# Four sets of priorities for a planned instruction order, and later planned arrivals, in a fused sparse attention and MoE kernel

## The chip, the cores and the metric

The kernel runs on one core of one Trainium2 chip. The core has five engines with their own instruction queues, each worked off in order: TensorE (PE; its weight loads are shown apart as PEld), VectorE (DVE), ScalarE (ACT), GpSimd (POOL) and SyncE (SP). They wait for each other and for DMA transfers by semaphores. In this kernel POOL and SP issue the transfers. The metric is the device time of one execution in microseconds, the median of several runs; lower is better.

## The reference

Inputs are q, k and v of shape (8, 8, 576, 64): batch, heads, positions, width. Then come an input matrix of 512 x 2048 and an output matrix of 2048 x 512, and two scalars s and b.

```python
scores = scale * np.matmul(q, k.transpose(0, 1, 3, 2))
mask_local = (rel >= 0) & (rel < 32)
mask_strided = (rel >= 0) & (pos[None, :] % 32 == pos[:, None] % 32)
# heads 0 to 3 are local, heads 4 to 7 strided; softmax; times v
x = attn_out.transpose(0, 2, 1, 3).reshape(4608, 512)
h = x @ w_in
r = np.maximum(h, 0.0)
out = (s * (r * r) + b) @ w_out
```

rel is the distance between query and key position. The output is 4608 x 512 in float32.

## The kernel before

**Tiling.** The eight batches are taken one after the other. Each has four pairs of heads, m = 0 to 3; m = 0 and 1 are local (suffix l, `loc`), m = 2 and 3 strided (suffix s, `str`). Because of the masks only small blocks of scores are computed: 6 blocks of 96 queries for a local pair, 8 of 72 for a strided one. For a pair, `pair_steps` (L474) makes the steps: transposes of q and k (`trans`, L485; from some batch on they are DMA transposes instead, L555 to L582), scores (L610), the exponential on ACT (L641), the mask on DVE (L649), the product with v (`av`, L673), the reciprocal of the row sums (L701), the scaling (L711) and the transpose of the result x (`xtrans`, L727, or DMA transposes, L752 to L763). The result is `xT`, one tile for each m, with room for three batches.

The tokens are then taken in nine blocks of 512, T = 0 to 8. FF1 (`ff1`, L973) multiplies xT with w_in, 16 tiles of 4 matmuls a block, followed by a relu (`u`, L1009 or L1011) and a square (`gT`, L1017 or L1019). FF2 multiplies gT with w_out (`ff2`, L1229, for T = 0 and 1; from T = 2 on `ff2_seven`, L853, with seven products of half blocks in place of eight, on sums of gT and of w_out, `S` and `w_mix`). For T = 7 and 8 FF1 too uses seven products (`ff1_seven`, L1087), on sums of xT (`x_sum`, L1036) and of w_in (`w_sum`), with the products kept by copies V, U and E (L1113).

**The order of the work** is not left to the hardware or a scheduler. While the kernel is built, the class `Plan` (L19) keeps a planned time `plan.t` and writes every engine's program in the order in which it plans the work. PE's work is a list of `Step`s with a planned duration each. Work of the other engines is *posted* when the step that it follows is planned: a post has needs (names of results), a cost for each engine that can do it ("A" ACT, "V" DVE, "P" POOL, "D", "X" and "Y" transfers on SP) and the names that it makes. `flush` (L45) takes from the posts that are ready at `plan.t` the one with the smallest key, and puts it on the engine that would finish it first:

```python
w = r + self.LATER.get(k[0] if isinstance(k, tuple) and k[2:3] != (0,) else None, 0.0)
```

r is the time at which its needs are there, k the first name that it makes, and `LATER` is the table `ORDER` (L124): a number of nanoseconds for each kind of name, by which it stands later (or, negative, earlier) in the choice. A post whose engines are all taken for more than `SLACK` (600 ns) beyond `plan.t` is held back. The kinds: q and k are the spreading and copying of transposed q and k (`qD_loc`, `qD_str`, `kT_loc`, `kTs`), e the exponential, p the mask (in batch 0, where a matmul adds the mask, p is the exponential), r the reciprocal, x the scaling, u the relu, g the square, `in` the copies that make loaded q, k and v usable, S, w_mix, wc and xc the sums, ev the output of FF2; the rest (Va to C22, fv to c12) belong to the seven-product forms.

**What PE does next** is chosen in the loop at L1520. Among four pairs of heads from the first unfinished one it takes the first whose next step is ready, and puts it ahead of FF1 and FF2 as long as the attention work done is below `due()` (L1515), which follows the positions reached in FF1 and FF2 plus `ahead`:

```python
pos = f1_pos[i1] + (f2[i2 - 1].pos if i2 else 0.0) + plan.ahead
return (pos if pos <= 1 else 1 + (pos - 1) / 2) * batch_ns
```

`batch_ns` is the planned PE time of one batch of attention (that of batch 1). FF1 goes before FF2 unless it is more than 1 block ahead (L1538). Where nothing is ready, early in the program, `keep_running` (L1487, matmul at L1502) fills PE's time with matmuls on constants; later the planned time is simply moved on. Real waits are kept by semaphores, so a wrong planned time can't change a result, only the order.

**Loads.** POOL issues the loads of inputs and weights. `landing` (L1309) plans when a load is there: it adds the loads up one after the other, and at the end 600 ns, or 6000 ns after 60 us. `fetch_qk` (L1319) loads q and k, `fetch_v` (L1339) v of a batch: `load_vl` the local heads into `v_loc`, `early_v` or `load_vs` the strided ones. v_loc is followed by a copy of 32 rows for each half of the heads (`rows_before`, L435, in the trace "v_loc<-v_loc" at L404).

Of the kernel before, what the change touches and what calls it, by code (L numbers as in the profile page):

```python
# [1 line left out]

# [1 line left out]

# [1 line left out]

# [12 lines left out]
class Plan:  # L19
# [8 lines left out]

    def __init__(self, order):
        self.t = 0.0  # L30
        self.SLACK, self.ahead, self.LATER = order["SLACK"], order["ahead"], order
        self.done = {}
        self.pend = []
        self.free = {"A": 0.0, "V": 0.0, "P": 7000.0, "D": 0.0, "X": 0.0, "Y": 0.0}
        self.banks = {}

    def ready_at(self, needs):
        if any(k not in self.done for k in needs):
# [3 lines left out]
    def post(self, needs, cost, fn, keys, lat=None):  # L42
        self.pend.append((needs, cost, fn, keys, lat))

    def flush(self):  # L45
        while True:
            best = None
            for p in self.pend:
                r = self.ready_at(p[0])
                if r is None or r > self.t:  # L50
                    continue
                if p[1].keys() <= {"A", "V"} and min(
                        self.free[e] for e in p[1]) > self.t + self.SLACK:
                    continue
                k = p[3][0]
                w = r + self.LATER.get(k[0] if isinstance(k, tuple) and k[2:3] != (0,) else None, 0.0)
                if best is None or w < best[0]:
                    best = (w, r, p)
            if best is None:
                return  # L60
            _, r, p = best
            self.pend.remove(p)
            eng = min(p[1], key=lambda e: max(self.free[e], r) + p[1][e])
            end = max(self.free[eng], r, self.t - self.SLACK) + p[1][eng]
            self.free[eng] = end
            p[2](eng)
            for k in p[3]:
                if isinstance(k, Group):
                    self.banks[k.name] = end + self.LAT[eng]
                    k = ("rel", k)  # L70
                soon = isinstance(k, tuple) and k[0] == "soon"
                self.done[k] = end + (6000.0 if soon else p[4] or self.LAT[eng])
# [45 lines left out]
class Step:  # L118
    def __init__(self, fn, ns, needs=(), group=None, keys=(), posts=(), after=None):
# [1 line left out]
        self.keys, self.posts, self.after = keys, posts, after  # L121


ORDER = {"g": 1500.0, "S": 2500.0, "in": 2500.0, "w_mix": 0.0, "wc": 1000.0, "ev": 1000.0,  # L124
         "c21": 1500.0, "c11": 500.0, "c12": 500.0, "C22": -1500.0, "fv": 0.0, "Vb": -400.0,
         "x": -1500.0, "Ub": 1000.0, "xc": -1500.0, "fe": -400.0, "k": 1500.0, "fu": -1500.0,
         "Va": 500.0, "p": 0.0, "c22": 500.0, "Ua": 2500.0, "e": -1500.0, "q": 0.0, "r": 0.0,
         "u": 0.0, "SLACK": 600.0, "ahead": 0.05}
KINDS = ("g", "S", "in", "w_mix", "wc", "Va", "Ua", "Ub", "Vb", "C22", "xc", "q", "k", "r", "x", "e",
         "p", "u", "ev", "fv", "fu", "fe", "c11", "c22", "c21", "c12")  # L130


def varied(order, rnd):

    order = dict(order)
    for kind in rnd.sample(KINDS, rnd.choice((1, 2, 4))):
        order[kind] = rnd.choice((-1500.0, -800.0, -400.0, 0.0, 500.0, 1000.0, 1500.0, 2500.0))
    if rnd.random() < 0.2:
        order["SLACK"] = rnd.choice((400.0, 600.0, 800.0, 1000.0))
    if rnd.random() < 0.2:  # L140
        order["ahead"] = rnd.choice((0.0, 0.05, 0.1, 0.2))
    return order


class Nothing:
# [11 lines left out]
        return self  # L157


ORDERS = 0  # L160


@with_exitstack
def kernel(
    ctx: ExitStack,
    tc: tile.TileContext,
    q: bass.AP,
    k: bass.AP,
    v: bass.AP,
    moe_w_in: bass.AP,  # L170
    moe_w_out: bass.AP,
    moe_s: bass.AP,
    moe_b: bass.AP,
    out: bass.AP,
):
    shapes = q.shape, out.shape, moe_w_in.shape
    nothing = [Nothing()] * 11
    rnd = random.Random(0)
    best = ORDER
    end = lay_out(*nothing, best, *shapes)  # L180
    for _ in range(ORDERS):
        other = varied(best, rnd)
        at = lay_out(*nothing, other, *shapes)
        if at < end:
            best, end = other, at
    lay_out(ctx, tc, tc.nc, q, k, v, moe_w_in, moe_w_out, moe_s, moe_b, out, best, *shapes)


def lay_out(ctx, tc, nc, q, k, v, moe_w_in, moe_w_out, moe_s, moe_b, out, order, q_shape, out_shape,
# [1119 lines left out]
    def landing(cost):  # L1309

        nonlocal ring
        ring = max(ring, plan.t + 2000.0) + cost

        return ring + (6000.0 if plan.t > 60000.0 else 600.0)

    def both(name, b):
        return [("in", name, b, mm) for mm in range(2)]
# [20 lines left out]

    def fetch_v(b):  # L1339
        load_vl(b)  # L1340
        plan.done["raw", "vl", b] = landing(4600)
        for mm in range(2):
            rows_before(b, mm, ("raw", "vl", b))
        if b < LONG_V:
            early_v(b)
        else:
            load_vs(b)
            arrive(both("vs", b), landing(5000))

    def early_v(b):  # L1350

# [162 lines left out]

    def due():  # L1515

        pos = f1_pos[i1] + (f2[i2 - 1].pos if i2 else 0.0) + plan.ahead
        return (pos if pos <= 1 else 1 + (pos - 1) / 2) * batch_ns

    while i2 < len(f2) or any(at_i[p] < len(att[p]) for p in range(len(att))):  # L1520
# [14 lines left out]
            order.append(1)  # L1535
        if i2 < len(f2):
            order.append(2)
        if len(order) == 2 and i1 % 4 == 0 and f1_pos[i1] > (f2[i2 - 1].pos if i2 else 0.0) + 1:  # L1538
            order.reverse()
        if i1 % 4:  # L1540
            order = [1]
# [54 lines left out]
```

## Time and profile before

| | |
|---|---|
| median of 4 runs | 298.18 us |
| lowest to highest | 297.76 to 300.17 us |
| the profiled execution's own time | 298.35 us |
| its span, first to last instruction | 296.5 us |
| mean granted clock of TensorE | 0.998 |
| bytes moved by transfers | 38.19 MB in 106153 packets |
| last load of the last batch issued, landed | 188.4 us, 201.3 us |
| first FF1 matmul (L983), first FF2 matmul (L1238) | 19.1 us, 38.2 us |
| last matmul of the attention products (L684) | 214.5 us |
| last matmul (L951), last store issued | 292.7 us, 293.5 us |

How to read it: times are from the span's start. The page gives busy time and instructions of each engine; groups of instructions by line, with mean duration and the idle time of their engine before them and who ended it; and the chain of work that ended last, followed back from the last instruction. A line of the waits names who waited, at which line, for whom, the total in us, how often, and the longest. A line of stretches gives the stretch, its length, the busy us and instructions of PE, PEld, DVE, ACT and POOL, the granted clock, the mean share of the DMA engines and GB/s. The ends of matmuls are modelled and overlap, so a full PE is better judged by the distance from one matmul's start to the next.

### The profile page before, as it was taken

The numbers are of one execution on the slowest core, as the hardware profiler recorded it, in microseconds if no ns is written. First come the engines' busy times: TensorE is split into PE (matmuls) and PEld (weight loads), VectorE is DVE, ScalarE is ACT, GpSimd is POOL, SyncE is SP. The second block draws the span as 40 slices with busy tenths as digits, with TensorE's granted clock in tenths as the row PEclk, the third lists the DMA queues.
The fourth block names the chain that finished last, engine by engine and source line by source line (L and its number), as shares of the span: only waits on it lengthen the run. The fifth ranks groups of instructions, "written<-read, shape, count | busy, mean of one in ns | idle before, by whom it ended". The sixth has DMA issues, their size and how long they took to land.

```text
span 296.5 us, 7092 instructions
## 1 busy us (share of the span) xinstructions
PE 290.2 (98%) x2802; PEld 219.5 (74%) x2802; DVE 236.0 (80%) x501; ACT 194.5 (66%) x336; POOL 93.6 (32%) x140
## 2 busy tenths in 40 slices
PE   8899999999999999999999999999999999999995
PEld 3775655666556558889767786678888989999984
DVE  5856888798976989777887896779898598888963
ACT  3577957898838698746774878388877545675400
POOL 8883623601990395009810394100000000000000
PEclk9999999999999999999999999999999999999999
DMA  8999999999999599999999899999530300210214
GB/s 128 196 206 203 216 176 181 209 178 138 118 185 152 73 130 135 158 171 127 154 143 189 126 168 115 95 161 215 65 97 0 108 34 4 71 38 3 97 47 143
DMA packets 106153, 38.19 MB, mean 129 GB/s; under 512 B 85415, under 2 KB 103975, under 8 KB 106119
## 3 DMA queue, kind: packets, MB, share of 16 engines
q0 software_dynamic: 60848, 18.23, 65.2%
q1 hardware_dynamic: 45270, 19.51, 37.9%
q8 instruction: 22, 0.36, 0.5%
q14 instruction: 13, 0.10, 0.1%
HBM read 36.99 MB, written 10.62 MB: 161 GB/s over the span
## 4 chain that ended last, share of the span: by engine, by line
PE 89%; POOL 3%; DMA 3%; ACT 2%; DVE 2%; issue 1%; SPq 0%; POOLq 0%
PE ps_f L983 32%; PE ps_f L951 23%; PE ps_f L1238 8%; PE ps_s L623 5%; PE ps_f L1208 3%; PE ps_a L684 3%; DMA qT<-qs 3%; PE ps_a L1208 2%; PE ps_t L1208 2%; PE ps_s L951 2%; PE ps_s L1208 2%; PE ps_t L951 1%; PE ps_s L1238 1%; PE ps_t L684 1%; PE ps_t L502 1%; PE ps_t L731 1%
## 5 line engine op out<-in xcount | busy, mean ns | idle before, releaser
L983 PE MATMUL ps_f<-xT,w_in_sb 128*128 128x512 f16 (+4 forms) x568 | 115.5, 331 | 0.0
L1009 ACT ACTIVATE u<-ps_f 128x512 f16<-128x512 f32 x104 | 61.0, 594 | 32.8 <-PE ps_f L983 32.1
L983 PEld LDWEIGHTS <-w_in_sb 128*128 128x128 f16 x576 | 57.3, 113 | 22.7
L951 PEld LDWEIGHTS <-gT 128*128 128x128 f16 x608 | 58.3, 98 | 9.2
L951 PE MATMUL ps_f<-w_out_sb,gT 128*128 128x256 f16 x376 | 55.6, 273 | 0.0
L1017 ACT ACTIVATE gT<-u 128x1024 f16<-128x1024 f16 x29 | 30.7, 1057 | 0.8
L1238 PE MATMUL ps_f<-w_out_sb,gT 128*128 128x512 f16 x112 | 30.4, 379 | 0.0
L951 PE MATMUL ps_f<-w_mix,gT 128*128 128x256 f16 x176 | 25.1, 273 | 0.0
L641 ACT ACTIVATE p_str<-ps_s 72x432 f16<-72x432 f32 (+1 forms) x46 | 20.7, 482 | 6.0 <-PE ps_s L623 5.4
L641 ACT ACTIVATE p_loc<-ps_s 128x384 f16<-128x384 f32 x46 | 21.4, 494 | 4.9 <-PE ps_s L623 4.4
L711 DVE TENSOR_TENSOR x_nat<-ps_a,rec 96x384 f16<-96x384 f32 (+2 forms) x46 | 24.0, 523 | 0.6
L819 DVE TENSOR_TENSOR gT<-gT 128x1024 f16<-128x1024 f16 x34 | 22.4, 679 | 0.9 <-ACT gT L1017 0.9
L1019 DVE TENSOR_TENSOR gT<-u 128x1024 f16<-128x1024 f16 x27 | 18.5, 686 | 3.7 <-ACT u L1009 3.2
L382 POOL DMA_DIRECT2D v_loc<-in_v_dram x24 | 17.6, 738 | 8.6 <-DMA w_out_sb<-in_moe_w_out_dram 5.2
L951 PEld LDWEIGHTS <-S 128*128 128x128 f16 x176 | 17.1, 98 | 2.9
L1238 PEld LDWEIGHTS <-gT 128*128 128x128 f16 x128 | 11.3, 98 | 7.8
L387 POOL DMA_DIRECT2D v_str<-in_v_dram x16 | 13.0, 817 | 12.9 <-DMA ks<-in_k_dram 4.7
L684 PEld LDWEIGHTS <-p_str 72*128 72x128 f16 x256 | 12.8, 97 | 5.2 <-ACT p_str L641 0.4
L1323 POOL COPY gate<-kT 1x1 f16<-1x1 f16 x6 | 1.8, 293 | 45.0 <-DMA kT<-ks 45.0
L951 PE MATMUL ps_f<-w_mix,S 128*128 128x256 f16 x112 | 15.5, 273 | 0.0
L701 DVE RECIPROCAL rec<-ps_a 96x6 f32<-96x6 f32 (+2 forms) x47 | 8.6, 182 | 8.1 <-PE ps_a L684 7.9
L1149 ACT ACTIVATE gT<-u 128x1024 f16<-128x1024 f16 x12 | 12.7, 1059 | 1.7 <-DVE u L1128 1.4
(237 smaller groups left out, 529.3 us busy)
## 6 DMA issues: line engine op xcount, KB each, us to landing
out_dram<-o SPq DMA_DIRECT2D x34, 256.0 KB, 2.7
w_in_sb<-in_moe_w_in_dram POOLq DMA_DIRECT2D x4, 512.0 KB, 9.8
w_out_sb<-in_moe_w_out_dram POOLq DMA_DIRECT2D x4, 512.0 KB, 9.4
qs<-in_q_dram POOLq DMA_DIRECT2D x6, 288.0 KB, 7.1
ks<-in_k_dram POOLq DMA_DIRECT2D x6, 288.0 KB, 9.2
v_loc<-in_v_dram POOLq DMA_DIRECT2D x24, 72.0 KB, 9.7
ql<-in_q_dram POOLq DMA_DIRECT2D x4, 288.0 KB, 9.2
kl<-in_k_dram POOLq DMA_DIRECT2D x16, 72.0 KB, 3.6
```

Of the source, the lines that this page charges most:

```text
L382: nc.gpsimd.dma_start(out=vl[LPAD:128, h, :, 0:D], in_=v_band(b, h))
L641: nc.scalar.activation(out=st["pw", g][0:nk, 0:2 * n * nq], in_=st["s", g][0:nk, 0:2 * n * nq], func=AF.Exp, scale=scale)
L684: nc.tensor.matmul(out=st["pa", g][:, n % 6, :], lhsT=st["pw", gp_][0:nk, i * nq:i * nq + WIDE], rhs=vt[0:nk, 2 * mm + e, j, :])
L711: nc.vector.tensor_tensor(out=x_at(0, cnt), in0=st["pa", g][0:nq, 0:cnt, 0:D], in1=st["rec", g][0:nq, 0:cnt].to_broadcast([nq, cnt, D]), o ...
L819: {"V": nc.vector, "P": nc.gpsimd}[eng].tensor_tensor(out=at(out), in0=at(x), in1=at(y), op=op)
L951: nc.tensor.matmul(out=gts[name, T, t][:, 0] if halves else gts[name, T][:, t], lhsT=lhs(k, t), rhs=rhs(k), start=fresh and k == 0 and (ha ...
L983: nc.tensor.matmul(out=gts["h", T, ft][:, lo:hi], lhsT=w_in_sb[ft // 4][:, ct].rearrange("p (x l) -> p l x", l=4)[:, ft % 4], rhs=xT[ct][: ...
L1009: nc.scalar.activation(out=u, in_=gts["h", T, ft], func=AF.Relu)
L1017: nc.scalar.activation(out=g, in_=u, func=AF.Square)
L1019: nc.vector.tensor_tensor(out=g, in0=u, in1=u, op=ALU.mult)
L1208: nc.tensor.matmul(out=st[bk][:, 256 * t:256 * t + 256], lhsT=lhs(t, c), rhs=rhs(c), start=fresh and t == c == 0, stop=t == c == 1, skip_g ...
L1238: nc.tensor.matmul(out=gts[id_], lhsT=gts[T][:, ft, ts * 128:(ts + 1) * 128], rhs=w_out_sb[:, ft, cols], start=(ft == 0), stop=(ft == NFT ...
```

## The change

`ORDER` becomes a list of four tables, and `UNTIL` says at which planned time each ends: 26, 110 and 215 us. Every lookup takes the table of the current planned time, for `SLACK` and `ahead` too. A new entry `lead` in each table (0.9, 1.1, 1.1, 0.9) takes the place of the 1 block that FF1 may be ahead of FF2. The lookup itself moves into `late`: for names that carry a pair of heads it first looks for an entry of that kind and pair, such as "k2" or "x0", and for loaded inputs of kind and half, such as "inql1"; only without one does the entry of the kind count, and then, as before, not for names whose third part is 0. All numbers in the tables are new. `SLACK` is 200, 600, 600 and 1000 ns, `ahead` 0.0, -0.2, -0.05 and -0.05.

`landing` adds 1600 ns in place of 600 for loads planned between 14 and 60 us. For the last batch the planned arrival of v, local and strided, is 5000 ns later. The function that varied the table, and the loop that could try variants (its count was 0), are gone; `flush` looks through the needs of a post in one loop, with the same outcome.

```diff
--- before.py
+++ after.py
@@ -1,6 +1,4 @@
 from contextlib import ExitStack
-
-import random
 
 import numpy as np
 
@@ -28,12 +26,20 @@
 
     def __init__(self, order):
         self.t = 0.0
-        self.SLACK, self.ahead, self.LATER = order["SLACK"], order["ahead"], order
+        self.orders = order
         self.done = {}
         self.pend = []
         self.free = {"A": 0.0, "V": 0.0, "P": 7000.0, "D": 0.0, "X": 0.0, "Y": 0.0}
         self.banks = {}
 
+    @property
+    def order(self):
+        return self.orders[sum(self.t >= x for x in UNTIL)]
+
+    @property
+    def SLACK(self):
+        return self.order["SLACK"]
+
     def ready_at(self, needs):
         if any(k not in self.done for k in needs):
             return None
@@ -42,20 +48,36 @@
     def post(self, needs, cost, fn, keys, lat=None):
         self.pend.append((needs, cost, fn, keys, lat))
 
+    def late(self, k, order):
+
+        if not isinstance(k, tuple):
+            return 0.0
+        at = k[1] if len(k) > 1 and isinstance(k[1], tuple) else k[2:4] if k[0] == "in" else ()
+        if len(at) == 2:
+            own = k[0] + (k[1] if k[0] == "in" else "") + str(at[1])
+            if own in order:
+                return order[own]
+        return 0.0 if k[2:3] == (0,) else order.get(k[0], 0.0)
+
     def flush(self):
+        order = self.order
+        slack = order["SLACK"]
         while True:
             best = None
             for p in self.pend:
-                r = self.ready_at(p[0])
-                if r is None or r > self.t:
-                    continue
-                if p[1].keys() <= {"A", "V"} and min(
-                        self.free[e] for e in p[1]) > self.t + self.SLACK:
-                    continue
-                k = p[3][0]
-                w = r + self.LATER.get(k[0] if isinstance(k, tuple) and k[2:3] != (0,) else None, 0.0)
-                if best is None or w < best[0]:
-                    best = (w, r, p)
+                r = 0.0
+                for k in p[0]:
+                    v = self.done.get(k)
+                    if v is None or v > self.t:
+                        break
+                    r = max(r, v)
+                else:
+                    if p[1].keys() <= {"A", "V"} and min(
+                            self.free[e] for e in p[1]) > self.t + slack:
+                        continue
+                    w = r + self.late(p[3][0], order)
+                    if best is None or w < best[0]:
+                        best = (w, r, p)
             if best is None:
                 return
             _, r, p = best
@@ -121,25 +143,48 @@
         self.keys, self.posts, self.after = keys, posts, after
 
 
-ORDER = {"g": 1500.0, "S": 2500.0, "in": 2500.0, "w_mix": 0.0, "wc": 1000.0, "ev": 1000.0,
-         "c21": 1500.0, "c11": 500.0, "c12": 500.0, "C22": -1500.0, "fv": 0.0, "Vb": -400.0,
-         "x": -1500.0, "Ub": 1000.0, "xc": -1500.0, "fe": -400.0, "k": 1500.0, "fu": -1500.0,
-         "Va": 500.0, "p": 0.0, "c22": 500.0, "Ua": 2500.0, "e": -1500.0, "q": 0.0, "r": 0.0,
-         "u": 0.0, "SLACK": 600.0, "ahead": 0.05}
-KINDS = ("g", "S", "in", "w_mix", "wc", "Va", "Ua", "Ub", "Vb", "C22", "xc", "q", "k", "r", "x", "e",
-         "p", "u", "ev", "fv", "fu", "fe", "c11", "c22", "c21", "c12")
-
-
-def varied(order, rnd):
-
-    order = dict(order)
-    for kind in rnd.sample(KINDS, rnd.choice((1, 2, 4))):
-        order[kind] = rnd.choice((-1500.0, -800.0, -400.0, 0.0, 500.0, 1000.0, 1500.0, 2500.0))
-    if rnd.random() < 0.2:
-        order["SLACK"] = rnd.choice((400.0, 600.0, 800.0, 1000.0))
-    if rnd.random() < 0.2:
-        order["ahead"] = rnd.choice((0.0, 0.05, 0.1, 0.2))
-    return order
+UNTIL = (26000.0, 110000.0, 215000.0)
+ORDER = [
+    {"g": 0.0, "S": -2500.0, "in": 500.0, "w_mix": 2500.0, "wc": 0.0, "ev": 2500.0, "c21": -200.0,
...
+     "Ua": -200.0, "e": -1500.0, "q": 500.0, "r": -800.0, "u": -2500.0, "SLACK": 200.0,
+     "ahead": 0.0, "p2": -800.0, "r3": 500.0, "inkl0": 2500.0, "q3": 1000.0, "lead": 0.9,
...
+    {"g": -1500.0, "S": -400.0, "in": 2500.0, "w_mix": 200.0, "wc": -800.0, "ev": -200.0,
...
+     "SLACK": 600.0, "ahead": -0.2, "r3": -200.0, "k1": 1500.0, "q1": -200.0, "invl1": -800.0,
+     "x2": -800.0, "x3": -2500.0, "lead": 1.1, "k3": 0.0, "p1": 0.0, "inql0": 2500.0,
...
+    {"g": 1500.0, "S": 2500.0, "in": 500.0, "w_mix": -800.0, "wc": 1000.0, "ev": 1000.0,
...
+     "u": 1500.0, "SLACK": 600.0, "ahead": -0.05, "lead": 1.1, "k1": -400.0, "inkl0": -400.0,
...
+    {"g": 200.0, "S": 200.0, "in": 200.0, "w_mix": 200.0, "wc": 1500.0, "ev": 1500.0,
...
+     "SLACK": 1000.0, "ahead": -0.05, "q0": 1500.0, "q1": 500.0, "invs1": -400.0, "x1": -800.0,
...
+     "invl0": -1500.0, "x2": -2500.0, "invs0": -2500.0, "k2": 200.0, "lead": 0.9, "p0": 1500.0,
...
+]
 
 
 class Nothing:
@@ -155,9 +200,6 @@
 
     def __getitem__(self, at):
         return self
-
-
-ORDERS = 0
 
 
 @with_exitstack
@@ -174,16 +216,7 @@
     out: bass.AP,
 ):
     shapes = q.shape, out.shape, moe_w_in.shape
-    nothing = [Nothing()] * 11
-    rnd = random.Random(0)
-    best = ORDER
-    end = lay_out(*nothing, best, *shapes)
-    for _ in range(ORDERS):
-        other = varied(best, rnd)
-        at = lay_out(*nothing, other, *shapes)
-        if at < end:
-            best, end = other, at
-    lay_out(ctx, tc, tc.nc, q, k, v, moe_w_in, moe_w_out, moe_s, moe_b, out, best, *shapes)
+    lay_out(ctx, tc, tc.nc, q, k, v, moe_w_in, moe_w_out, moe_s, moe_b, out, ORDER, *shapes)
 
 
 def lay_out(ctx, tc, nc, q, k, v, moe_w_in, moe_w_out, moe_s, moe_b, out, order, q_shape, out_shape,
@@ -1311,7 +1344,7 @@
         nonlocal ring
         ring = max(ring, plan.t + 2000.0) + cost
 
-        return ring + (6000.0 if plan.t > 60000.0 else 600.0)
+        return ring + (6000.0 if plan.t > 60000.0 else 1600.0 if plan.t > 14000.0 else 600.0)
 
     def both(name, b):
         return [("in", name, b, mm) for mm in range(2)]
@@ -1338,14 +1371,15 @@
 
     def fetch_v(b):
         load_vl(b)
-        plan.done["raw", "vl", b] = landing(4600)
+        late = 5000.0 if b == B - 1 else 0.0
+        plan.done["raw", "vl", b] = landing(4600) + late
         for mm in range(2):
             rows_before(b, mm, ("raw", "vl", b))
         if b < LONG_V:
             early_v(b)
         else:
             load_vs(b)
-            arrive(both("vs", b), landing(5000))
+            arrive(both("vs", b), landing(5000) + late)
 
     def early_v(b):
 
@@ -1514,7 +1548,7 @@
 
     def due():
 
-        pos = f1_pos[i1] + (f2[i2 - 1].pos if i2 else 0.0) + plan.ahead
+        pos = f1_pos[i1] + (f2[i2 - 1].pos if i2 else 0.0) + plan.order["ahead"]
         return (pos if pos <= 1 else 1 + (pos - 1) / 2) * batch_ns
 
     while i2 < len(f2) or any(at_i[p] < len(att[p]) for p in range(len(att))):
@@ -1535,7 +1569,7 @@
             order.append(1)
         if i2 < len(f2):
             order.append(2)
-        if len(order) == 2 and i1 % 4 == 0 and f1_pos[i1] > (f2[i2 - 1].pos if i2 else 0.0) + 1:
+        if len(order) == 2 and i1 % 4 == 0 and f1_pos[i1] > (f2[i2 - 1].pos if i2 else 0.0) + plan.order.get("lead", 1.0):
             order.reverse()
         if i1 % 4:
             order = [1]
```

## The prediction, made before the result was known

> **What bounds the kernel now.** I read the page's first part, then the waits of TensorE, then its busy time by stretches, then the chain of work that ended last. The first part says that PE is the engine to watch:
>
> ```profile
> PE 290.2 (98%) x2802; PEld 219.5 (74%) x2802; DVE 236.0 (80%) x501; ACT 194.5 (66%) x336; POOL 93.6 (32%) x140
> ```
>
> 98% could still hide slack, because one matmul's modelled time overlaps the next. The chain of work settles it: there, 17 matmuls of 512 columns (L983) take 3.67 us, 216 ns from start to start, and all later pieces keep that pace (4 take 0.86 to 0.87 us). So from 20.6 us on PE streams almost without a hole. All waits that the trace shows for PE are these:
>
> ```profile
> PE ps_s L1502 <- DVE w_mix L316: 1.1, 1, 1.1
> PE ps_f L623 <- DVE kTs L404: 0.5, 1, 0.5
> PE ps_f L684 <- ACT p_str L641: 0.3, 1, 0.3
> PE ps_a L1208 <- ACT E L404: 0.2, 1, 0.2
> PE ps_a L494 <- DMA kl<-in_k_dram: 0.2, 1, 0.2
> PE ps_f L684 <- POOL v_loc L404: 0.2, 1, 0.2
> ```
>
> Each line: who waited, for whom, total us, times, longest. 2.5 us in all, and 1.1 of it before the first load can have come. The busy time by stretches (length, then busy us of PE, PEld, DVE, ACT, POOL) shows where PE is not full:
>
> ```profile
> 5.30:13.00 7.70, 7.29 (x122) 5.51 (x122) 4.92 (x20) 3.77 (x12) 7.48 (x13) 1.00 1.39 190
> 13.00:20.60 7.60, 6.67 (x126) 5.64 (x123) 5.74 (x20) 5.78 (x19) 6.76 (x12) 1.00 1.24 206
> ...
> 200.00:220.00 20.00, 19.85 (x230) 16.73 (x229) 18.07 (x44) 17.14 (x28) 0.00 (x0) 1.00 0.67 126
> 220.00:240.00 20.00, 19.76 (x182) 17.72 (x181) 15.17 (x32) 12.00 (x19) 0.00 (x0) 1.00 0.17 55
> ```
>
> Every other stretch from 20.6 to 280 us is full. In the head some of the busy time is filler (L1502, matmuls on constants that keep_running puts where nothing is ready). The same stretches for L1502 alone:
>
> ```profile
> 5.30:13.00 7.70, 2.36 (x17) 1.11 (x16) 1.00 1.39 190
> 13.00:20.60 7.60, 0.55 (x4) 0.30 (x4) 1.00 1.24 206
> ```
>
> So an order of work can win back, at most: 7.60 - 6.67 + 0.55 = 1.48 us between 13 and 20.6 us; 0.15 + 0.24 = 0.39 us between 200 and 240 us; and 7.70 - 7.29 + 2.36 = 2.77 us between 5.3 and 13 us. The last is held by landings: ql at 5.27 and 7.70, kl at 6.96 and 8.49, qs at 9.94, ks at 11.86 us, and no load of batch 0 is issued otherwise by this change. The tail is fixed too: the last matmul starts at 292.7, its DVE step at 293.02 takes 0.48, the last store leaves at 293.53 and the span ends at 296.5.
>
> **Part by part.** The change adds and removes no computing instruction. It moves posts (evictions, masks, exponentials, copies) in the queues of DVE and ACT, chooses between the two for some, moves steps in PE's program, and can drop fillers. PE's useful matmuls stay the same, and so do their 216 ns.
>
> *The priorities of the first stretch (up to 26 us planned).* Here the gain must come from. At 14.56 PE waited 0.53 us for kTs: on DVE that copy (14.05, 0.46) stood behind x_nat of pair 0 (12.62, 0.55) and the two halves of qD_str (13.10, 0.91). At 18.68 PE waited for the exponentials p_str (18.10, 0.82), whose scores came late (ACT idle 0.91 before). Both are questions of order, 0.5 + 0.3 us by the waits above. Unknown is whether the new order does better: below, it gives back nothing and a kTs copy that falls behind one more x_nat costs 0.55; above, all 1.48. I take 0.8, the two waits named.
>
> *The stretches after it.* Between 26 and 200 us PE has nothing to gain; orders can only cost. At 204 us PE shows a hole of 0.15 in the stretch sums, at 238 one of 0.24 behind the copy E. I take half of 0.39, 0.2. Priorities also choose the engine: the square (L1017 ACT 1057 ns, L1019 DVE 686) is the largest such choice, and DVE has 40 - 35.26 = 4.7 us free between 240 and 280, ACT 16.6, so there it is DVE whose order matters.
>
> *ahead and lead.* Attention runs while its work done is under due(). Once past position 1, a change of ahead moves due by half of it, in batches. A batch of attention is 2 x (480 + 560 + 528 + 544 + 420 + 560 + 210 + 280) = 7,164 ns of planned PE time by the step costs in the code. ahead goes from 0.05 to -0.2 in the second stretch, 0.125 of a batch, 0.90 us of work. The fetches of ql start at 73.7, 101.9, 134.3 and 168.6 us, 31.6 apart in the mean, so attention comes about 3.9 us later there, and in the third and fourth (0.05 to -0.05) 0.05 x 31.6 = 1.6 us later. The work that fills is FF1 and FF2, which PE has in plenty. lead swaps FF1 and FF2 by 0.1 of a block; same cover, 0.
>
> *1000 ns more for loads planned between 14 and 60 us.* It delays users in PE's, ACT's and DVE's programs, not the loads. The row that it bears on is at 46.09 us, where v of batch 1 landed at 46.07:
>
> ```profile
> ACT v_loc L404 <- DMA v_loc<-in_v_dram: 1.4, 1, 1.4
> ```
>
> ACT was blocked 1.45 us with the sums of b (46.77) queued behind; PE was full throughout. So the wait may go and the time won is 0; if it stays, 0.
>
> *5000 ns more for v of batch 7.* Its copies into the band rows stood on DVE at 192.1 and on ACT at 193.04, after a landing at 192.95; the products that read them start at 201.5, those of v_str (last landing 201.31) at 207.4. Cover for the first is about 7 us. For the second, what follows is x_out and the transposes (216.7, 219.2), the sums x_sum of block 7 (DVE, 223.0 to 223.9) and their first matmul at 230.08: 6.2 us. The 5.0 fits; with the 1.6 of ahead it is 6.6, which would cost 0.4 if both came fully. I take 0, and keep 0.4 for the range.
>
> Sum: 0.8 + 0.2 = 1.0 us. The profiled run took 298.35 us, 1.85 around its span of 296.5, and lies 0.17 over the median of 298.18; so 297.35 on its own scale, 297.2 against the median.
>
> **Two rules of the skill against rows.** The Trainium skill, "TensorE: Matmul & The Clock Gate", section "Back-to-back issue gap", gives two figures for 512 columns, some 216 ns alone and some 131 ns sustained in a stream with weight loads; by the second, the 448 matmuls of 512 columns in FF1 and FF2 would hold 448 x 0.085 = 38 us that a better order could win. The row says 216 ns in just such a stream, so I count none of it. The same page, section "Part 1: The HAM clock gate", says that an idle window of some 3.4 us halves the clock; in this trace the granted clock is 1.00 in every stretch up to 280 us and no hole reaches 0.7 us, so no run here shows it, and it would only make the rival below that stalls some 1.7 us dearer.
>
> **Rivals.**
>
> *Nothing moves (298.2).* Batch 0 is bound by its landings and by POOL's casts of v_str (15.06, 2.28 us, after vs landed at 14.91), so what the new order wins at 14.5 is lost at 17 to 18. For it: POOL is busy 6.76 of 7.60. Against it: x of the last pair is only ready at 22.25, 4.9 us after the casts.
>
> *A late transfer blocks ACT (301.5): the other side.* The last batch has no margin. The chain of work that ended last leaves PE there, and only there after 21 us for more than a copy:
>
> ```profile
> 193.14 0.88 PE ps_f L983 x4
> 194.02 0.02 issue
> 194.04 0.61 ACT u L1009
> 194.65 0.37 SPq L582
> 195.01 0.05 issue
> 195.07 7.53 DMA qT<-qs
> 202.60 0.02 issue
> 202.62 0.67 ACT qD_str L404
> 203.29 0.01 issue
> 203.30 0.67 ACT qD_str L404
> ```
>
> The transpose took 7.53 us where its group lands in 3.1 in the median. ACT and DVE wait 1.01, 0.58, 0.70 and 0.24 us for such transfers between 193 and 203. Behind the waiting copy stand evictions of FF1 (u, 0.60 each), and PE waits for those once its two f1 banks are full, 2 x 0.86 = 1.7 us. If the new order puts a copy 5 us too early, PE loses 5.0 - 1.7 = 3.3. It decides from 1.7 us of extra lateness. Against it: attention there is 1.6 us later by ahead, which adds margin if the issues don't slip as much.
>
> *The DVE-heavy end loses its order (299.1).* DVE is busy 35.26 of 40 us from 240 on. If each of the 8 units of the seven-product FF1 takes one wait like that for E (0.24), that is 1.9; less the 1.0, +0.9.
>
> *More is won (294.9).* All 1.48 + 0.39, and half of the 2.77 before 13 us: 3.3.
>
> **Numbers.** Forecast 297.2: 0.48. Nothing moves, 298.2: 0.22. Late transfer, 301.5: 0.13. DVE at the end, 299.1: 0.12. More, 294.9: 0.05. The range 295.6 to 300.6 leaves out the third and the last, 0.18; it holds the full 1.87 (296.3), a part of what lies before 13 us, and above it the 0.55 and 0.4 with the 299.1 and a late transfer of up to 4 us. 1% is 3.0 us, about what a measurement of this kernel can tell from no change: faster by more takes the last case or a little of the forecast's edge, 0.06; slower by more takes the late transfer, 0.14; the rest 0.80.
>
> **What would show it.** Right: fewer L1502 or less PE idle time between 13 and 20.6 us, the dense L983 stream starting about 0.8 us earlier and every later landmark (first L1238 at 38.2, first L1208 at 228.2, last L951 at 292.7) earlier by as much; no line for v_loc among ACT's waits near 46 us. Wrong: new PE waits on ACT or DVE between 190 and 240 us, or between 26 and 190, where now there are none; a last batch whose x reaches FF1 after 228 us; PE busy under 20 in any stretch of 20 us from 240.

## The result, and the profile after

| | before | after |
|---|---|---|
| median of all runs | 298.56 us (69 runs) | 297.41 us (43 runs) |
| lowest to highest | 297.74 to 300.82 | 297.04 to 299.11 |
| ratio to before | | 0.9965, 95% interval 0.9955 to 0.9975 |
| profiled execution, its span | 298.35, 296.5 us | 297.26, 295.5 us |
| first FF1 matmul | 19.05 us (L983) | 18.25 us (L1016) |
| first FF2 matmul | 38.20 us (L1238) | 38.02 us (L1271) |
| first seven-product FF1 matmul | 228.23 us (L1208) | 229.27 us (L1241) |
| last matmul | 292.71 us (L951) | 292.04 us (L984) |

The change makes the kernel about 1.0 us faster. The interval of the ratio doesn't reach 1.000, though single runs of one kernel differ by more than the gain. The ratio weighs all runs and is not the quotient of the medians (0.9961). One run of e3 and one of e12 below (305.39 and 304.46 us), more than 1.5% above the fastest run of the same kernel, are left out of medians and ratios. The lines of the code stand 33 or 34 lower in the kernel after: L983 is L1016, L951 is L984, L1208 is L1241, L404 is L437, the filler L1502 is L1536.

First the page of the kernel after: busy time (its part 1), and the shares of the chain that ended last (its part 4).

```profile
PE 289.1 (98%) x2800; PEld 218.9 (74%) x2800; DVE 236.0 (80%) x498; ACT 194.6 (66%) x334; POOL 93.0 (31%) x140
PE 95%; POOL 3%; DVE 1%; issue 1%; ACT 0%; POOLq 0%
```

The busy share of PE has not moved; it can't tell the two kernels apart. The chain can. Before, it was

```profile
PE 89%; POOL 3%; DMA 3%; ACT 2%; DVE 2%; issue 1%; SPq 0%; POOLq 0%
```

and its 3% of DMA was the last batch's transpose; after, the chain stays on PE to the end. All waits of PE in the kernel after (who, for whom: total us, times, longest):

```profile
PE ps_s L1536 <- DVE w_mix L349: 1.1, 1, 1.1
PE ps_t L527 <- DMA ql<-in_q_dram: 0.9, 1, 0.9
PE ps_f L717 <- DVE v_loc L437: 0.7, 1, 0.7
PE ps_f L717 <- POOL v_loc L437: 0.5, 1, 0.5
```

The waits for kTs (0.5), p_str (0.3) and E (0.2) are gone; in the head waits for two copies of v_loc have come (0.7 and 0.5, where before there was one of 0.2). The same four stretches as in the prediction (length, then busy us of PE, PEld, DVE, ACT, POOL, clock, DMA share, GB/s):

```profile
5.30:13.00 7.70, 6.93 (x114) 5.15 (x115) 4.73 (x19) 3.76 (x7) 7.39 (x13) 1.00 1.40 188
13.00:20.60 7.60, 6.83 (x130) 5.79 (x127) 6.26 (x20) 5.77 (x17) 6.22 (x11) 1.00 1.23 204
200.00:220.00 20.00, 20.00 (x234) 17.24 (x232) 17.56 (x43) 15.98 (x27) 0.00 (x0) 1.00 0.58 128
220.00:240.00 20.00, 20.00 (x186) 18.00 (x184) 17.01 (x35) 11.99 (x19) 1.64 (x1) 1.00 0.16 49
```

And the fillers alone (L1536):

```profile
5.30:13.00 7.70, 2.33 (x14) 1.00 (x14) 1.00 1.40 188
13.00:20.60 7.60, 0.55 (x4) 0.25 (x4) 1.00 1.23 204
```

Between 200 and 240 us PE is full now. Between 13 and 20.6 us it is busy 0.16 us more, with the same 0.55 us of fillers: much less than the 0.8 that was forecast.

**Where the time went.** Busy time is too coarse for a microsecond in 296, so I add up PE's lost time: for each matmul the distance to the next one's start, less what it takes in a dense stream (0.417 ns a column and 3.5 ns, 217 ns for 512 columns; for float32 twice as much a column); a filler counts in full. Where small matmuls run side by side the figure is negative, so only differences between kernels mean something. Beside the two profiles stand those of the same kernels run again (e1 and e2 below), which tell what belongs to a program and what to one execution.

| stretch, us | before | before again | after | after again |
|---|---|---|---|---|
| 0 to 5.3 | 4.27 | 4.42 | 4.53 | 4.27 |
| 5.3 to 13 | 2.54 | 2.28 | 2.43 | 2.49 |
| 13 to 20.6 | 2.28 | 2.28 | 1.81 | 1.81 |
| 20.6 to 60 | -2.67 | -2.67 | -2.25 | -2.25 |
| 60 to 160 | -0.40 | -0.40 | -0.23 | -0.23 |
| 160 to 195 | -0.02 | -0.02 | -0.17 | -0.17 |
| 195 to 210 | 0.32 | 1.30 | -0.09 | 0.97 |
| 210 to 245 | 0.10 | 0.10 | -0.29 | -0.29 |
| 245 to last matmul | -0.44 | -0.44 | -0.43 | -0.44 |
| last matmul's start to the end | 3.79 | 3.78 | 3.45 | 3.67 |

From 13 to 195 us, and from 210 us to the last matmul, each kernel repeats itself to 0.01 us. The sum of the differences of the two first profiles is 0.26 - 0.11 - 0.47 + 0.42 + 0.17 - 0.15 - 0.41 - 0.39 + 0.01 - 0.34 = -1.01; the spans differ by 1.0. So:

- **The head** gains 0.47 between 13 and 20.6 us, but 0.42 is lost again by 60 us. Both are one piece of work, the product of s and b with the sums. Before, it ran in the head (timeline of PE):

```profile
16.43 0.38 PE L1294 MATMUL ps_f<-sb_row,w_mix 1*128 1x2 f32 x2
```

From start to start its two matmuls take 0.31 us, and with the pauses where PE goes over to them and back, 0.42. After, the same 0.42 stand in the full stream:

```profile
22.12 0.43 PE ps_f L1016 x2
22.55 0.31 PE ps_f L1327 x2
22.86 0.55 PE ps_s L1016 x2
```

These are pieces of the chain of the kernel after (start, length, what). The holes of the head itself changed by 0.05. The 0.17 lost between 60 and 160 us I could put down to no single instruction.
- **The late holes.** The hole behind the copy E cost 0.40 us, and another one at 175 us 0.15. Both are gone. The timeline of PE before (start, length, line, tiles, and in brackets the idle time and who ended it):

```profile
237.83 0.60 PE L1208 MATMUL ps_a<-qD_loc,ks 128*128 128x256 f16 x4
238.27 0.60 PE L1208 MATMUL ps_s<-xT,w_in_sb 128*128 128x256 f16 x4
239.11 0.60 PE L1208 MATMUL ps_a<-xT,v_str 128*128 128x256 f16 x4 [0.24 <-ACT E L404]
```

and after:

```profile
238.00 0.60 PE L1241 MATMUL ps_s<-xT,w_in_sb 128*128 128x256 f16 x4
238.44 1.91 PE L984 MATMUL ps_f<-w_out_sb,gT 128*128 128x256 f16 x16
240.18 0.60 PE L984 MATMUL ps_f<-w_mix,gT 128*128 128x256 f16 x4
240.62 0.60 PE L1241 MATMUL ps_t<-xT,v_str 128*128 128x256 f16 x4
```

Four matmuls come every 0.43 or 0.44 us; before, 0.84 us lie between 238.27 and 239.11, so the hole is 0.40 and not the 0.24 of the bracket, which counts from a modelled end. After, 20 matmuls of FF2 stand in that place.
- **Between 195 and 210 us** each kernel can lose anything from nothing to over 1 us, by when the last batch's transfers land.
- **The end** is 0.34 us shorter. There SP waits for the last stores to land; before and after:

```profile
SPq L1591 <- DMA out_dram<-o: 1.2, 3, 0.6
SPq L1625 <- DMA out_dram<-o: 0.9, 2, 0.6
```

The last store leaves 0.82 us after the start of the last matmul in both, but the one ahead of it 0.16 after that start before the change, and 0.05 ahead of it after. This belongs to the programs: the end takes 3.45 to 3.48 us in the kernel after and in e6 and e8, and 3.78 to 3.83 in before, e1, e3, e4, e5, e7, e9 and e10. In the second profile of after it takes 3.67 us: the store leaves as early, but the last step on DVE waited 0.60 us for an earlier store of its buffer. Which entry of the tables does it was not tried.

Without the stretches that depend on landings (up to 13 us, and 195 to 210), the rows add up to -0.75 us, near the 0.70 by which the lowest times differ.

### The profile page after: what moved, and what is told of

It reads as the page before. It is cut to its first block, busy times and chain, and to the rows that moved or that the text cites. A ratio compares the mean times of both kernels' runs of the same rounds, so it can differ in the third digit from the quotient of the medians.

```text
span 295.5 us, 7100 instructions
## 1 busy us (share of the span) xinstructions
PE 289.1 (98%) x2800; PEld 218.9 (74%) x2800; DVE 236.0 (80%) x498; ACT 194.6 (66%) x334; POOL 93.0 (31%) x140
## 4 chain that ended last, share of the span: by engine, by line
PE 95%; POOL 3%; DVE 1%; issue 1%; ACT 0%; POOLq 0%
PE ps_f L1016 32%; PE ps_f L984 25%; PE ps_f L1271 8%; PE ps_s L656 5%; PE ps_f L1241 3%; PE ps_a L717 3%; PE ps_t L1241 2%; PE ps_s L984 2%; PE ps_a L1241 2%; PE ps_s L1241 2%; PE ps_t L717 1%; PE ps_t L984 1%; PE ps_s L1271 1%; PE ps_f L717 1%; PE ps_t L535 1%; PE ps_f L535 1%
## 5 line engine op out<-in xcount | busy, mean ns | idle before, releaser
L1016 PE MATMUL ps_f<-xT,w_in_sb 128*128 128x512 f16 (+4 forms) x568 | 115.3, 331 | 0.0
L1042 ACT ACTIVATE u<-ps_f 128x512 f16<-128x512 f32 x107 | 62.8, 595 | 34.5 <-PE ps_f L1016 31.9
L1016 PEld LDWEIGHTS <-w_in_sb 128*128 128x128 f16 x576 | 57.1, 114 | 23.1
L984 PEld LDWEIGHTS <-gT 128*128 128x128 f16 x608 | 58.3, 98 | 8.6
L984 PE MATMUL ps_f<-w_out_sb,gT 128*128 128x256 f16 x376 | 53.4, 273 | 0.0
L1271 PE MATMUL ps_f<-w_out_sb,gT 128*128 128x512 f16 x112 | 31.9, 379 | 0.0
L1052 DVE TENSOR_TENSOR gT<-u 128x1024 f16<-128x1024 f16 x32 | 21.8, 683 | 5.2 <-ACT u L1042 4.8
L1050 ACT ACTIVATE gT<-u 128x1024 f16<-128x1024 f16 x24 | 25.4, 1058 | 0.7
L984 PE MATMUL ps_f<-w_mix,gT 128*128 128x256 f16 x176 | 24.9, 273 | 0.0
L674 ACT ACTIVATE p_loc<-ps_s 128x384 f16<-128x384 f32 x46 | 20.7, 489 | 5.9 <-PE ps_s L656 5.4
L744 DVE TENSOR_TENSOR x_nat<-ps_a,rec 72x384 f16<-72x384 f32 (+2 forms) x45 | 23.6, 524 | 0.6
L984 PEld LDWEIGHTS <-S 128*128 128x128 f16 x176 | 17.1, 98 | 2.8
L717 PEld LDWEIGHTS <-p_str 72*128 72x128 f16 x256 | 13.6, 98 | 5.8 <-ACT p_str L674 0.7
L1271 PEld LDWEIGHTS <-gT 128*128 128x128 f16 x128 | 11.4, 98 | 6.9 <-issue 0.2
L734 DVE RECIPROCAL rec<-ps_a 72x6 f32<-72x6 f32 (+2 forms) x45 | 8.3, 184 | 9.1 <-PE ps_a L717 8.8
L984 PE MATMUL ps_f<-w_mix,S 128*128 128x256 f16 x112 | 15.0, 273 | 0.0
L717 PEld LDWEIGHTS <-p_loc 128*128 128x128 f16 x192 | 11.1, 98 | 5.0 <-ACT kTs L437 0.8
```

The costliest lines, as they stand in the source:

```text
L674: nc.scalar.activation(out=st["pw", g][0:nk, 0:2 * n * nq], in_=st["s", g][0:nk, 0:2 * n * nq], func=AF.Exp, scale=scale)
L717: nc.tensor.matmul(out=st["pa", g][:, n % 6, :], lhsT=st["pw", gp_][0:nk, i * nq:i * nq + WIDE], rhs=vt[0:nk, 2 * mm + e, j, :])
L744: nc.vector.tensor_tensor(out=x_at(0, cnt), in0=st["pa", g][0:nq, 0:cnt, 0:D], in1=st["rec", g][0:nq, 0:cnt].to_broadcast([nq, cnt, D]), o ...
L984: nc.tensor.matmul(out=gts[name, T, t][:, 0] if halves else gts[name, T][:, t], lhsT=lhs(k, t), rhs=rhs(k), start=fresh and k == 0 and (ha ...
L1016: nc.tensor.matmul(out=gts["h", T, ft][:, lo:hi], lhsT=w_in_sb[ft // 4][:, ct].rearrange("p (x l) -> p l x", l=4)[:, ft % 4], rhs=xT[ct][: ...
L1042: nc.scalar.activation(out=u, in_=gts["h", T, ft], func=AF.Relu)
```

## The experiments

Two explanations stood against each other. One: the gain is fixed, a matter of the instruction order, either in the head (as predicted) or behind the copy E. The other: it lies in the last batch, whose transfers land differently from run to run, and which the new arrivals plan later. A third question was whether the tables, the arrivals and ahead each bring their part by themselves. Ratios are to the kernel before on the same chip, with 95% intervals.

**The two kernels again, unchanged.**

> The kernel before, unchanged, to see which holes of its profile come back. If the gain of the change lies in the late holes: TensorE again shows about 0.15 us idle time between 200 and 220 us and 0.24 between 220 and 240, and some 1.5 us idle time and filler between 13 and 20.6 us. If the late holes were chance: they are gone here and the last matmul starts near 292.0. Ratio 1.000 with 0.001 either way.

> The changed kernel, unchanged. If the gain lies in the late holes: TensorE is full between 200 and 240 us again, the dense stream of FF1 after the head starts no earlier than before (useful matmul work done by 26 us within 0.3 us of before), ratio 0.9965. If the head gives the gain as predicted and the profile at hand only caught a late first landing: work done by 26 us is 0.8 us ahead of before.

Before again: 299.00 us in the median (10 runs), 1.0019 (0.9994 to 1.0043). The head and the hole behind E came again as they were. New was what happened at 196 us. This is the chain that ended last of that run:

```profile
177.05 0.71 POOL v_loc L382
177.76 0.01 issue
177.77 17.81 DMA v_loc<-in_v_dram
195.58 0.02 issue
195.60 0.02 ACTq L404
195.62 0.04 issue
195.66 0.12 ACT v_loc L404
195.78 0.51 issue
196.28 0.59 ACT u L1009
196.88 0.04 issue
196.92 1.02 PE ps_f L983 x4
```

and ACT's timeline there:

```profile
195.66 0.72 ACT L404 COPY v_loc<-v_loc 32x640 f16<-32x640 f16 x1 [2.75 <-DMA v_loc<-in_v_dram]
```

v_loc landed at 195.58 us, in the first profile at 192.95. Its copy held ACT for 2.75 us, the eviction u stood behind it, and PE lost 0.79 us at 196.0 behind u and 0.58 at 200.2 behind p_loc, another of ACT's results. That is the mechanism of the rival with the late transfer, already at work in the kernel before.

After again: 297.48 us (10 runs), 0.9957 (0.9925 to 0.9988). Here too the last batch lost time, in another place. Stretch and wait of that profile, which took 298.43 us, far above the median:

```profile
200.00:220.00 20.00, 19.14 (x225) 16.25 (x223) 16.51 (x40) 15.14 (x26) 0.00 (x0) 1.00 0.49 119
```

```profile
PE ps_s L656 <- DMA kT<-ks: 0.9, 1, 0.9
```

The transpose of k took 8.50 us, from 195.80 to 204.30, and cost PE 1.03. So the full 200 to 220 us of the first profile after is not the program's doing, and a single profile can't be used for that stretch.

**The first table alone; all but the first table.**

```diff
 ORDER = [
     {"g": 0.0, "S": -2500.0, "in": 500.0, "w_mix": 2500.0, "wc": 0.0, "ev": 2500.0, "c21": -200.0,
...
-    {"g": -1500.0, "S": -400.0, "in": 2500.0, "w_mix": 200.0, "wc": -800.0, "ev": -200.0,
+    {"g": 1500.0, "S": 2500.0, "in": 2500.0, "w_mix": 0.0, "wc": 1000.0, "ev": 1000.0, "c21":
...
```

In e3 the second to fourth tables are the one table of before, and the planned arrivals too are those of before. In e4 it is the other way round: the table of before for the first stretch, everything else as after.

> The first of the four tables as changed, the other three as before, planned arrivals as before. If the head gives the gain as predicted: about 0.8 us less, ratio 0.997, and the work done by 26 us is 0.8 us ahead. If the gain lies late: ratio 1.000 with up to 0.002 either way, head work as before, and the holes between 195 and 240 us stay or change at random, since every later step moves with the first stretch.

> The first table as before, the other three and both planned arrivals as changed. If the gain lies late: the holes between 195 and 240 us are gone, ratio 0.996 to 0.997. If the head gives the gain: ratio 0.999 to 1.000, at most 0.2 us less.

e3: 302.58 us (3 runs), 1.0182 (1.0125 to 1.0238). e4: 300.48 us (6 runs), 1.0069 (1.0048 to 1.0090). Both are slower than either kernel, and no theory had expected it. In e3 the lost time from 13 to 20.6 us is the 1.81 of the kernel after, but other holes open. The longest waits of PE behind the head, of e3:

```profile
PE ps_a L702 <- DVE p_loc L667: 1.0, 1, 1.0
PE ps_f L969 <- DVE o L900: 0.5, 1, 0.5
```

and of e4:

```profile
PE ps_t L528 <- ACT xT L430: 1.1, 1, 1.1
PE ps_f L977 <- DVE Va L896: 0.8, 1, 0.8
PE ps_s L1234 <- DVE qD_loc L1109: 0.7, 1, 0.7
```

None of these is in before or after. A table for one stretch changes what is planned at every later time, and PE, full from 20.6 us on, pays for each post that comes too late.

**The last table alone**, with the other three and the arrivals as before, so that up to 215 us planned the programs are those of before:

```diff
...
-    {"g": 1500.0, "S": 2500.0, "in": 500.0, "w_mix": -800.0, "wc": 1000.0, "ev": 1000.0,
+    {"g": 1500.0, "S": 2500.0, "in": 2500.0, "w_mix": 0.0, "wc": 1000.0, "ev": 1000.0, "c21":
...
     {"g": 200.0, "S": 200.0, "in": 200.0, "w_mix": 200.0, "wc": 1500.0, "ev": 1500.0, "c21": -400.0,
```

> Only the fourth table (planned time from 215 us) as changed; every program is the one before up to that time. Theory A, a fixed part in the last stretch: the TensorE hole of 0.4 us at 238 to 239 us (behind the copy E) goes, no new hole comes, ratio 0.9985 to 0.999. Rival B, all of the gain is fewer waits on the last batch's transfers between 195 and 210 us, which this leaves as they are: ratio 1.000, and the hole stays or is paid elsewhere in the stretch.

297.88 us (12 runs), 0.9974 (0.9955 to 0.9993). Its stretch from 220 us is full, where before it was 19.76:

```profile
220.00:240.00 20.00, 20.00 (x186) 18.03 (x184) 15.97 (x33) 11.98 (x19) 2.25 (x1) 1.00 0.18 56
```

PE's lost time from 210 to 245 us is -0.30 as after (-0.29), before 0.10. So 0.40 of the gain is the last table's, by the order alone.

**v of the last batch not planned later**, the rest as after:

```diff
-        late = 5000.0 if b == B - 1 else 0.0
+        late = 0.0
```

> The changed kernel without the 5000 ns for v of the last batch. If the later planned arrival protects against the transfers of the last batch: ACT or DVE waits for v_loc near 193 to 197 us, TensorE holes of 1 us or more between 195 and 210 us, ratio 1.000 to 1.004 against before. If it only shifts copies under cover, as predicted: ratio 0.9965 as with it, holes between 195 and 210 us as in the changed kernel (0 to 1 us).

297.91 us (10 runs), 0.9967 (0.9944 to 0.9990). By this ratio it can't be told from after; but its lowest time, 297.67 us, is 0.63 above after's, and 27 of after's 43 runs lie below it. In its profile ACT waited 1.98 us for v_loc at 195.4 us, without a hole on PE. What PE lost is elsewhere, in the order:

```profile
PE ps_s L1241 <- DVE qD_loc L1116: 0.4, 1, 0.4
```

This is the first matmul on x_sum, at 230.0 us; start to start the hole is 0.60, about as much as the lowest times differ by. So neither expectation came true: no hole between 195 and 210 us, and yet the 5000 ns are worth about half a microsecond in this order.

**Both kernels without the loads of v of the last batch.**

```diff
     def load_vl(b):
+        if b == B - 1: return
...
     def load_vs(b):
+        if b == B - 1: return
```

> The kernel before, but v of the last batch is not loaded (the products of batch 7 use an older v; all instructions but those 8 transfers stay). If the transfers of the last batch are what stretches the 195 to 210 us part by 0.3 to 1.3 us: the transposes there get through sooner, that part shows under 0.1 us of holes, ratio 0.996 to 0.998. If they are not: ratio 0.9995 to 1.000.

> The changed kernel, but v of the last batch is not loaded. If the gain is fixed holes plus fewer waits for the last batch's transfers: against the kernel before without that v only the fixed part is left, 0.4 us, so ratio about 0.9945 to 0.9965 against before, and 195 to 210 us without holes. If the change gains nothing but less waiting for transfers, both kernels without v take the same time.

Before without: 298.04 us (10 runs), 0.9975 (0.9956 to 0.9994), and no run over 298.36. After without: 297.48 us (10 runs), 0.9955 (0.9938 to 0.9972). The two stretches of before without these loads:

```profile
200.00:220.00 20.00, 20.00 (x234) 17.16 (x232) 18.41 (x44) 17.14 (x28) 0.00 (x0) 1.00 0.34 81
220.00:240.00 20.00, 19.76 (x183) 17.75 (x181) 15.18 (x33) 12.19 (x18) 0.00 (x0) 1.00 0.16 51
```

With the loads gone the loss before 220 us goes and the hole behind E stays: the two are separate. Taking the loads away gives the kernel before some 0.5 us in the median (298.04 against 298.57 beside it) and the kernel after nothing in the median (297.48; with the loads 297.41 to 297.48). But after has late runs too: 13 of its 43 lie above the highest without the loads (297.84), as 40 of the 69 of before lie above 298.36. What is left between the two without the loads, 0.56 us by the medians and 0.65 by the lowest times, is the fixed part.

**v of the last batch planned later, alone and with the last table.** e9 is the kernel before with only the 5000 ns; e10 has the fourth table as well.

```diff
-        plan.done["raw", "vl", b] = landing(4600)
+        late = 5000.0 if b == B - 1 else 0.0
+        plan.done["raw", "vl", b] = landing(4600) + late
...
-            arrive(both("vs", b), landing(5000))
+            arrive(both("vs", b), landing(5000) + late)
```

> The kernel before with the 5000 ns for v of the last batch as the only edit; the programs are those before up to the copy of v_loc on ACT near 193 us, which moves behind several evictions. Theory: this copy, blocked by a late v_loc, is what makes the kernel before lose 0.3 to 1.3 us between 195 and 210 us in some runs: no wait of ACT for v_loc, spread of the runs down to 0.5 us, ratio 0.9975 to 0.9985; the hole at 239 us stays (0.40). Rival: the waits there come from the transposes on SP whatever ACT does: spread and median as before, ratio 0.9995 to 1.0005.

> The fourth table and the 5000 ns together, the rest as before. If the gain is these two: no hole at 239 us, no ACT wait for v_loc, ratio 0.996 to 0.997, as the whole change. If the other tables matter, or if parts that were planned apart make new holes: 0.998 or more, with a hole of its own between 210 and 245 us.

e9: 299.62 us (12 runs), 1.0041 (1.0023 to 1.0059). e10: 300.00 us (10 runs), 1.0058 (1.0034 to 1.0082). Planned later by itself, v makes the kernel slower, and e9 had been expected to be faster. ACT no longer waits for v_loc in the last batch, as expected, but what follows is late. In e9:

```profile
PE ps_s L1241 <- DVE qD_loc L1116: 0.8, 1, 0.8
```

and in e10:

```profile
PE ps_s L1241 <- DVE qD_loc L1116: 1.6, 1, 1.6
```

It is the wait for x_sum that the prediction had named as the end of the cover; start to start the holes are 0.93 at 230.5 us and 1.76 at 230.7 us. e9 has three more from 203 to 205 us, of 0.20 to 0.25 each.

**After with the arrivals of the second and third batch as before.**

```diff
-        return ring + (6000.0 if plan.t > 60000.0 else 1600.0 if plan.t > 14000.0 else 600.0)
+        return ring + (6000.0 if plan.t > 60000.0 else 600.0)
```

> The changed kernel with 600 ns in place of 1600 for loads planned between 14 and 60 us. If the later arrivals only take waits from ACT and DVE, as predicted, and the order fits either way: ratio 0.9965, ACT waiting for v_loc near 46 us again (about 1 us), TensorE full there. If the later tables fit only the start they were planned with: new holes of 0.4 us or more after 60 us, ratio 1.000 or more.

299.87 us (10 runs), 1.0043 (1.0028 to 1.0059). ACT waits again 0.9 us for v_loc near 46 us, and PE has waits that after has not:

```profile
PE ps_f L984 <- DVE Va L903: 0.6, 1, 0.6
PE ps_f L1271 <- DVE gT L1052: 0.3, 1, 0.3
```

They lie at 146 and 82 us, far from the wait near 46 us, at which PE stays full. The end, too, takes 4.39 us.

**After with ahead and lead as before**, in all four tables:

```diff
-     "ahead": 0.0, "p2": -800.0, "r3": 500.0, "inkl0": 2500.0, "q3": 1000.0, "lead": 0.9,
+     "ahead": 0.05, "p2": -800.0, "r3": 500.0, "inkl0": 2500.0, "q3": 1000.0, "lead": 1.0,
...
```

> The changed kernel with ahead 0.05 and lead 1 in all four tables, as before. If ahead matters as margin for the last batch: attention comes earlier, the last batch's products at 199 to 201 us or before, holes between 195 and 210 us, ratio 1.000 to 1.005. If it is of no weight in itself, and only any part replaced alone does harm: holes anywhere after 60 us, ratio above 1.000, with the stretch from 195 to 210 us no worse than 1 us.

300.73 us (9 runs), 1.0087 (1.0051 to 1.0123). PE waits:

```profile
PE ps_s L656 <- DMA kT<-ks: 1.1, 1, 1.1
...
PE ps_f L1271 <- ACT gT L1050: 0.9, 1, 0.9
```

and the hole of 0.40 behind E is back, though the last table's priorities are those of after. Neither expectation fits alone: a hole of 1.04 us opens at 82.6 us, as if any part replaced did harm, but 195 to 210 us loses 1.21, nearly all of it at kT, where after again lost 1.03 without the edit. The products of the last batch start at 201.70 us, not at 199 to 201.

## Why the prediction was right in its number, and where its steps were wrong

The forecast was 297.2 us; 297.41 was measured. The sum of 1.0 us came out, but not by its own terms: 0.8 of it was not there, and gains that the prediction did not count or called fixed took its place. That the number is right is in good part luck.

- **The head, 0.8 us: this term was mis-sized.** The lost time fell by 0.47, but 0.42 of that is the product of s and b, which is paid for in the full stream at 22.5 us instead, so the head is worth about 0.05. The dense FF1 stream did start 0.80 us earlier, as predicted, but "every later landmark earlier by as much" failed at once: the first FF2 matmul came 0.18 earlier. The step that failed is adding up two waits as if nothing would take their place; both went (0.5 and 0.3), and waits for v_loc on DVE and POOL came (0.7 and 0.5, of which 0.2 had been there). And the prediction looked for fillers as the only work that could go, not for useful work that only moves.
- **The late holes, half of 0.39.** The hole of 0.24 behind E was really 0.40 from start to start, and all of it went; with the one at 175 us, which the busy sums had hidden, that is 0.55 us. The e5 run shows the 0.40 to come from the last table alone. The hole of 0.15 at 204 us, though, was one execution's: before again had 1.30 us of lost time in that place and before without the loads of v none.
- **The end, called fixed,** is 0.34 us shorter, by the store before the last.
- **The last batch** was treated as a risk only. The lowest times of the two kernels are 0.70 us apart (297.74 and 297.04), their medians 1.15. Medians lie above the lowest by 0.82 before and by 0.37 after; without the loads of v by 0.29 (before, 298.04 less 297.75) and 0.38 (after). So before, the late landings cost the median run about half a microsecond, and after, where fewer runs are late, they hardly do. What in the change does it is open: e5, whose programs equal those of before until 215 us planned, has 0.41 in its 12 runs, which speaks against the later arrivals as the only cause, and e6 without the 5000 ns has 0.24.
- **ahead and lead, 0:** the cover held in the kernel after. The shift was smaller than the 1.6 us of the prediction: the first product on v_loc of the last batch starts at 202.14 us, before at 201.46. With the old values put back alone (e12) the kernel loses some 3 us, of which the wait for kT may be chance. That doesn't contradict the 0, since the tables were left as they are, but it shows that 0 is no property of ahead by itself.
- **Loads planned 1000 ns later, 0:** the wait of ACT for v_loc near 46 us is gone, as forecast, and e11 shows it coming back with the old arrivals while PE stays full there. The 2.5 us that e11 loses lie at other places.
- **5000 ns for v, 0 with 0.4 in reserve:** no cost in the kernel after, but not 0 either: without them (e6) a hole of 0.60 us opens, so there they gain. And the cover of 6.2 us was read from an order in which the copies run when v lands; in the order of e9 the same 5000 ns cost 1.2 us (1.0041 of 298.29), most of it at the very matmul named. The path was right; whether the cover holds depends on the rest of the order.
- **The rivals.** A change that does nothing is out by the interval. The late transfer is real, but in both kernels: its threshold of 1.7 us can be tried on before again, where 2.75 us of blocking would give 1.05 of loss by the prediction's subtraction and 1.37 was lost in two holes, with ACT busy without a pause from one to the other. At the DVE-heavy end nothing changed, -0.44 and -0.43 from 245 us on. Of the wider gain, the 2.77 us before 13 us stayed with the landings. Of the signs named for being right, the FF1 stream and the wait for v_loc came true, the later landmarks not: the first FF2 matmul came 0.18 earlier, the first seven-product one 1.04 later, the last one 0.67 earlier.

**The parts taken singly.** The prediction priced each edit by itself and added up. Of the eight kernels with only a part of the set, six (e3, e4, e9 to e12) are slower than before, by 0.4 to 1.8%; in their profiles the holes open at places that the exchanged part doesn't name. The other two, e5 and e6, lie between the two kernels in the median (297.88 and 297.91 us), with intervals that overlap that of after. So the prices don't add up: each holds only for the rest of the order that it was read from. No kernel that computes everything had a lower median than the one after.

**The two rules.** PE's pace never came near the 131 ns that the Trainium skill's "TensorE: Matmul & The Clock Gate", section "Back-to-back issue gap", gives for a sustained stream: in the kernel after, 23 FF1 matmuls of 512 columns take 4.96 us, 216 ns each, with weight loads between. And the longest hole after the head was 1.76 us (e10, mean granted clock 1.000), so no run here shows what the section "Part 1: The HAM clock gate" says of idle windows of some 3.4 us. The traces do show another pace at the very start: in the kernel before, the fillers of 512 columns from 1.45 to 4.87 us stand 427 ns apart, twice the later 216, though the rows of stretches give the granted clock as 1.00 there.

## What to carry to other kernels

Where one engine's stream is full, judge a new order by the distances from start to start over the whole program, and count useful work that only moves from one stretch to another as no gain. Run a kernel twice under the profiler before a hole is read as the program's: here the holes that came again to 0.01 us were the order's, and the others followed the landings of transfers. Priorities and planned times of a static order are one set: a part of them alone made this kernel slower in six cases of eight.

## What was not expected of the hardware

The loads of v_loc of the last batch, the same four in the same program, took 13.4 to 14.9 us to land in one execution and 13.9 to 17.8 us in another, so that the last landed at 192.95 and at 195.58 us; the transpose of k into kT took up to 8.50 us (e2). The copy that waits for the last of them stands in ACT's queue ahead of an eviction, and from 195 to 210 us TensorE lost 0.32 us in the one execution and 1.30 in the other. By contrast, the lost time of each stretch between 13 and 195 us came again to 0.01 us.
